# Order in which weight tiles are converted during the first output products, and the place of the first expert gather

## The chip, the cores and the metric

The kernel runs on one core of one Trainium2 chip. The metric is device time in microseconds for one execution, lower is better. TensorE (PE in the profile, PEld for its weight loads) does the matrix products, VectorE (DVE) and ScalarE (ACT) elementwise work, GpSimd (POOL) elementwise work on SBUF and indirect DMAs, and SyncE (SP) issues most of the direct DMAs. Each engine takes its instructions in a fixed order.

## The reference

Three parts in a row, all in float32:

```python
# attention over 32 memory slots: q, k, v [4, 8, 576, 64], phi [4, 8, 576, 32]
a = exp(phi - max over seq); a = a / (sum over seq + 1e-9)
k_m, v_m = einsum('bhsm,bhsd->bhmd', a, k), einsum('bhsm,bhsd->bhmd', a, v)
x = softmax(q @ k_m^T / 8) @ v_m          # then laid out as 2304 tokens x 512
# gated layer: w_gate, w_val [512, 1536], w_out [1536, 512], stored as float64
x = (silu(x @ w_gate) * (x @ w_val)) @ w_out
# experts: r_gate [512, 8], w1 [8, 512, 1024], w2 [8, 1024, 512]
e = argmax(x @ r_gate); each token goes to expert e, in order of tokens, up to its capacity
out = softmax weight of e * (relu(x @ w1[e]) @ w2[e]), zero where the capacity is used up
```

The three weights of the gated layer arrive as 64-bit numbers and have to be turned into pairs of 32-bit numbers on the chip (a high part and the rest). Every product is made of three passes over such pairs.

## The kernel before

**Groups of the gated layer.** The 1536 columns of the gated layer are 12 tiles of 128 (`ft` 0 to 11), in three thirds of four. The four batches are two pairs: LATE (2, 3) and (0, 1). The work is done in six groups (L61, L62): LATE with the first third, LATE with the second, (0, 1) with the first, (0, 1) with the second, (0, 1) with the last, LATE with the last. This text calls them group 0 to group 5. A group (`moe_group`, L1081) has an input phase of eight steps, one for each tile and batch (`moe_in`, PE L652, with the gate on ACT L660 and DVE L661 and L662, and its split into a pair on ACT L118 and POOL L122), and then the output products (`moe_out`, PE L673), four runs of four columns of products, with the result copied (L681) or added (L683) to `yp`. Before the steps of a tile its weights are multiplied with the attention memories (`mem_in`, PE L609 and L624, pair made on ACT L118 and DVE L122).

**Conversion of a weight tile.** `prep_load` (L540) loads the two raw halves of a tile of `w_gate` and `w_val` (512 KB each, SP, tag `wr` with four buffers, so two tiles). `split64` (L141) converts one half: ACT L149, DVE L150, L152 and L153, ACT L118, POOL L122. The result lies in a buffer of tag `w8` (five buffers, 1 MB each). The tiles of `w_out` go the same way (`out_load` L574, `out_made` L583; six tiles `o0` to `o5`, two for each third). A converted tile is also stored to DRAM (`wsc`, `osc`), because a later group needs it again; it is then loaded back by a POOL DMA (`prep_back` L569 at L571, `prep_out` L591 at L596).

**Which tile when.** `prep_to(i)` (L1058) makes tiles in the order of the groups, and loads the raw halves of the next one ahead. Group 0 converts tiles 0 to 3 and `o0`, `o1` in its input phase. During its output products it makes tile 4 (L1170), loads the raw halves of tile 5, and then (L1174 to L1181) converts tile 7, `o3` and `o2`, which are stored, let go and loaded back in group 1. Tiles 5 and 6 are converted in group 1.

**Order on the engines.** The instructions are put in order by a planner, which simulates the engines and takes, of the instructions that it thinks ready, the one that is earliest in the program, or has been given a higher priority. `behind()` (L127) opens a block in which each DVE or ACT instruction is put after the last gate made so far. `prep_made` (L561) and `out_made` use it for every conversion. The chip then follows that order, with its own times.

**Routing and experts.** In group 5 (and 4) each finished block of 288 tokens is routed (`route`, L690): logits, argmax, position; POOL scatters the token numbers to `perm` (L753) and SP stores the rows to `x2` (L779). At the start of group 5 `end_of_first` (L1211) finishes the routing of the four early blocks, makes a table of two full units of 288 tokens (`unit_table`), starts loading the first expert's weights and reads the token numbers of both units (`unit_slots`, L839). After the output products of the first LATE batch, in a `behind()` block, `begin_early` (L1199) makes the row indices (`slots_of`, DVE L850 and L851), gathers the first unit's 3 x 96 rows from `x2` (`unit_gather`, POOL L863), transposes them (`unit_x`, PE L911), converts expert weights and gathers the second unit. The rows of block 4 are stored to `x2` before this in the program, those of blocks 5 to 7 after it. Then the units follow (`unit_up` PE L925, `unit_down` PE L951).

Of the kernel before, what the change touches and what calls it, by code (L numbers as in the profile page):

```python
# [21 lines left out]
def attention_moe_moe_kernel(  # L22
# [27 lines left out]
    NDT = DM // 128  # L50
# [29 lines left out]
    def w8(shape, name, dt=F32R):  # L80
        return sb.tile(shape, dt, tag="w8", name=name, bufs=5)
# [45 lines left out]
    def behind():  # L127

        stack = ExitStack()
        for ins in last:  # L130
            stack.enter_context(tc.issue_after(ins.ins))
        return stack
# [107 lines left out]
    def advance(gen, n):  # L240
        for _ in range(n):
            if gen is None or next(gen, StopIteration) is StopIteration:
                return
# [296 lines left out]
    def prep_load(ft):  # L540
        raws = []
        for src in (w_gate, w_val):
            raw = wraw([128, NDT, 128, 2], "wr", I32)
            nc.sync.dma_start(
                raw.rearrange("p t f w -> p (t f w)"),
                src[:, ft * 128 : ft * 128 + 128].bitcast(I32).rearrange("(t p) f -> p t f", p=128),
            )
            raws.append(raw)
        return raws
# [9 lines left out]
    stored = set()  # L559

    def prep_made(ft, w, raws):  # L561
        with behind():
            for i in range(2):
                advance(prep_split(w, raws, i), ALL)
        if ft >= FG:
            prep_store(ft, w)
        return w
# [6 lines left out]
    def out_load(t):  # L574
        raws = []
        for i in range(2):
            raw = wraw([128, DM, 2], "wor", I32)
            r0 = (2 * t + i) * 128
            nc.sync.dma_start(raw.rearrange("p f w -> p (f w)"), w_out[r0 : r0 + 128].bitcast(I32))
            raws.append(raw)  # L580
        return raws

    def out_made(t, raws):  # L583
        w = w8([128, 2, 2, DM], "wo")
        with behind():
            for i in range(2):
                advance(split64(raws[i], w[:, i, 0], w[:, i, 1]), ALL)
        nc.sync.dma_start(osc[t].bitcast(F32), w.rearrange("p i a f -> p (i a f)").bitcast(F32))
        return w
# [269 lines left out]
    def unit_gather(st, slots):  # L859
        st["idx"], idg = slots  # L860
        xr = st["xr"] = txr([CH, NC, ROW], "xr")
        for c in range(NC):
            nc.gpsimd.indirect_dma_start(  # L863
                xr[:, c], None, x2, bass.IndirectOffsetOnAxis(idg[:, c : c + 1], 0)
            )
# [215 lines left out]
    def moe_group(g, gen):  # L1081

        bs, G = PAIRS[g], GROUPS[g]
        start = g == 0
        rt = None
        ghs = [[], []]
        fts = range(G * FG, (G + 1) * FG)
        if start:
            steps = [(i, ft) for i in range(2) for ft in fts]
        else:  # L1090
            steps = [(i, ft) for ft in fts for i in range(2)]
        ws = []
        first = g * FG
        mhs = {}

        jobs = {2: [8, 9, ("o", 4)], 3: [10, 11, ("o", 5)]}.get(g, [])
        job_raws = {}
        prep_to(first + (0 if start else LOOK))
        low = not start

        def memory(n):
            i, ft = steps[n]
            w = preps[first + ft - G * FG]
            if start:
                mhs[n] = first_mh.pop() if first_mh else mem_in(bs[0], w, (i,))[0]
            elif i == 0:
                mhs[n], mhs[n + 1] = mem_in(bs[0], w, (0, 1))

        memory(0)
        for n, (i, ft) in enumerate(steps):  # L1110
            if n + 1 < len(steps) and start:
                if n < FG:
                    prep_to(steps[n + 1][1])
                if n + 1 == FG:
                    advance(gen, ALL)
                    gen = both(0)
                    low = True
                memory(n + 1)
            if n + 3 >= len(steps) and len(ws) < 2:
                ws.append(prep_out(2 * G + len(ws)))  # L1120
            ghs[i].append(moe_in(bs[i], mhs.pop(n), g > 1))
            if start and i == 1:
                prep_store(ft, preps[ft])
            if not start and n + 2 < len(steps):
                memory(n + 2)
            if i == 1 and not start:
                prep_to(min(first + ft - G * FG + 1 + LOOK, first + FG))
            if n % 2 == 0 and n // 2 < len(jobs):
                job = jobs[n // 2]
                job_raws[job] = prep_load(job) if isinstance(job, int) else out_load(job[1])  # L1130
            if n % 2 == 1 and n // 2 < len(jobs):
                job = jobs[n // 2]
                if isinstance(job, int):
                    prep_made(job, w8([128, 2, NDT, 2, 128], "wgv"), job_raws[job])
                else:
                    out_made(job[1], job_raws[job])
                stored.add(job)
            with tc.high_priority(offset=50 if low else 0), (behind() if start and low else ExitStack()):
                advance(gen, 3 if (start and not low) or g == 5 else 1)
        if g == 1:  # L1140
            for i, b in enumerate(LATE):
                nc.sync.dma_start(asc[i].bitcast(F32), state[b]["at"].rearrange("p q a t -> p (q a t)").bitcast(F32))
        if g == 1:
            for i in range(NT // 128):
                pin(nc.sync.dma_start(
                    out[i * 128 : (i + 1) * 128].rearrange("p (t c) -> p t c", t=NDT),
                    zero.unsqueeze(1).to_broadcast([128, NDT, 128]),
                ))

            for i in range(NT // 256, NT // 128):  # L1150
                pin(nc.sync.dma_start(
                    x2[i * 128 : (i + 1) * 128, :DM].rearrange("p (t c) -> p t c", t=NDT),
                    zero.unsqueeze(1).to_broadcast([128, NDT, 128]),
                ))
                pin(nc.sync.dma_start(x2[i * 128 : (i + 1) * 128, DM:], zero[:, : ROW - DM]))
        if g == 4:
            for i, b in enumerate(LATE):
                at = state[b]["at"] = tb([128, 2, 2, 2 * NB], "at")
                nc.sync.dma_start(at.rearrange("p q a t -> p (q a t)").bitcast(F32), asc[i].bitcast(F32))
        if g == 5:  # L1160
            for i, b in enumerate(LATE):
                yps[b] = tb([128, 2, NDT, NB], "yp", F32)
                nc.sync.dma_start(yps[b].rearrange("p n d t -> p (n d t)"), ysc[i])
            advance(gen, ALL)
        for j, b in enumerate(bs):
            if G == 0:
                yps[b] = tb([128, 2, NDT, NB], "yp", F32)
            for n in range(2):
                if 2 * j + n < LOOK:
                    prep_to(first + FG + 2 * j + n)  # L1170
                for _ in moe_out(G, ghs[j], ws, yps[b][:, n], n):
                    advance(rt, 1)
                advance(rt, ALL)
                k = 2 * j + n - 1  # L1174
                if start and k == 0:
                    prep_made(2 * FG - 1, w8([128, 2, NDT, 2, 128], "wgv"), prep_load(2 * FG - 1))
                    stored.add(2 * FG - 1)
                elif start and k > 0:
                    t = 3 - (k - 1)
                    out_made(t, out_load(t))  # L1180
                    stored.add(("o", t))  # L1181
                with tc.high_priority(offset=50):
                    advance(gen, 1)
                if G == NG - 1:
                    rt = route(2 * b + n, yps[b][:, n])
            if g == 5 and j == 0:
                with behind():
                    begin_early()
            if g == 1:
                nc.sync.dma_start(ysc[j], yps[b].rearrange("p n d t -> p (n d t)"))  # L1190
        if g > 0:
            advance(gen, ALL)
        return rt, gen
# [2 lines left out]
    early = []  # L1196
    first_unit = []

    def begin_early():  # L1199
        slots = early.pop()  # L1200
        early.append(slots_of(slots, "e"))
        st = first_unit.pop()
        unit_gather(st, early[1][0])
        unit_x(st)
        unit_w1(st, 3)
        early.append(st)
        st = unit_begin(early[0], 1)
        unit_gather(st, early[1][1])
        early.append(st)
# [95 lines left out]
```

## Time and profile before

| what | value |
|---|---|
| time, median of 3 runs | 840.52 us (839.5 to 840.86) |
| time of the profiled execution | 835.02 us |
| span of its profile | 833.3 us |
| PE busy | 708.3 us, 85% of the span |
| DVE, ACT, POOL busy | 60%, 44%, 31% |

Times of the trace are microseconds from the start of the span. A row of a timeline gives the start, the duration, the engine, the line, the operation with its tiles, and in brackets how long the engine had been idle and what ended it. The granted clock is that of TensorE, as a share of its full 2.4 GHz.

### The profile page before, as it was taken

To read this page: it belongs to the slowest core of one execution; us is meant where nothing else is said; L and a number is where in the kernel's file an instruction comes from. 1 tells how busy PE (TensorE), PEld (TensorE's weight loads), DVE (VectorE), ACT (ScalarE), POOL (GpSimd) and SP (SyncE) were. 2 spreads that over 40 slices of the span, in tenths; PEclk is the share of its full clock that TensorE was granted. 3 is DMA by queue.
4 is the path that set the end of the run, shared out by engine and by line. 5 is a ranking of instruction groups with operands and counts; after the bars stand their busy time and mean duration, and the time that the engine had idled before them with its cause. 6 is when DMAs were issued, how large, how long until landed. Compare 5 with 4: busy or idle time off the path is not lost. (4 is left out here: it accounts for less than half of the span.)

```text
span 833.3 us, 14158 instructions
## 1 busy us (share of the span) xinstructions
PE 708.3 (85%) x5232; PEld 672.3 (81%) x5232; DVE 502.6 (60%) x1100; ACT 370.0 (44%) x763; POOL 254.2 (31%) x289
## 2 busy tenths in 40 slices
PE   6777689921889988988999999959699999999992
PEld 5557679911779978987999988949599999999992
DVE  4767868547645685187275687746446675547551
ACT  2444455424642465365073465426135544544440
POOL 1453353034622164055042154041134222111101
PEclk7767989975989999999999999979889999999997
DMA  9958299998951179067164498442329666546521
GB/s 231 239 173 219 76 274 347 295 217 280 373 163 57 58 274 332 2 208 297 54 217 147 107 190 161 152 138 62 69 76 339 245 207 208 187 162 205 181 77 31
DMA packets 91672, 152.69 MB, mean 183 GB/s; under 512 B 28815, under 2 KB 66319, under 8 KB 84816
## 3 DMA queue, kind: packets, MB, share of 16 engines
q1 hardware_dynamic: 83712, 113.68, 46.6%
q0 software_dynamic: 7888, 38.07, 14.5%
q8 instruction: 43, 0.70, 0.4%
q14 instruction: 29, 0.24, 0.1%
HBM read 111.48 MB, written 40.51 MB: 182 GB/s over the span
## 5 line engine op out<-in xcount | busy, mean ns | idle before, releaser
L673 PE MATMUL py<-gh,wo 128*128 128x288 f32 x1152 | 163.7, 298 | 3.7 <-DVE sg L661 3.0
L673 PEld LDWEIGHTS py<-gh,wo 128*128 128x128 f32 x1152 | 155.4, 188 | 6.0 <-DVE sg L661 3.5
L652 PE MATMUL pg<-at,mh 128*128 128x288 f32 x576 | 109.0, 316 | 20.8 <-DVE sg L661 8.6
L122 POOL TENSOR_TENSOR gh<-sg,gh 128x288 fp32r<-128x288 f32 x96 | 81.0, 855 | 112.6 <-ACT gh L118 112.2
L925 PE MATMUL p<-xt,w1h 128*128 128x288 f32 x768 | 111.8, 301 | 0.6 <-DVE hh L120 0.6
L652 PEld LDWEIGHTS pg<-at,mh 128*128 128x128 f32 x576 | 88.4, 200 | 28.6 <-DVE sg L661 9.8
L652 PE MATMUL pv<-at,mh 128*128 128x288 f32 x576 | 105.7, 309 | 4.9 <-DVE sg L662 4.1
L951 PE MATMUL p<-hh,w2h 128*128 128x288 f32 x768 | 108.4, 298 | 0.0
L925 PEld LDWEIGHTS p<-xt,w1h 128*128 128x128 f32 x768 | 104.9, 191 | 1.6 <-DVE hh L120 0.8
L951 PEld LDWEIGHTS p<-hh,w2h 128*128 128x128 f32 x768 | 103.1, 188 | 0.6 <-ACT w2h L118 0.3
L652 PEld LDWEIGHTS pv<-at,mh 128*128 128x128 f32 x576 | 89.2, 199 | 6.4 <-DVE sg L662 5.0
L122 DVE TENSOR_TENSOR w2h<-w2r,w2h 128x1024 fp32r<-128x1024 f32 x36 | 42.4, 1220 | 57.6 <-ACT w2h L118 56.5
L122 DVE TENSOR_TENSOR mh<-pm,mh 64x512 fp32r<-64x512 f32 (+1 forms) x92 | 63.1, 688 | 22.3 <-ACT mh L118 20.5
L661 DVE SCALAR_TENSOR_TENSOR sg<-sg,pg 128x288 f32<-128x288 f32 x96 | 42.2, 449 | 51.5 <-ACT sg L660 50.6
L624 PE MATMUL pm<-wgv,tv 128*128 128x256 f32 x288 | 43.9, 301 | 33.9 <-ACT wgv L118 33.7
L660 ACT ACTIVATE sg<-pg 128x288 f32<-128x288 f32 x96 | 38.2, 409 | 71.1 <-PE pg L652 51.4
L624 PEld LDWEIGHTS pm<-wgv,tv 128*128 128x128 f32 x288 | 39.7, 203 | 35.5 <-ACT wgv L118 33.9
L118 ACT ACTIVATE mh<-pm 64x512 fp32r<-64x512 f32 (+1 forms) x92 | 54.4, 592 | 27.9 <-PE pm L624 16.6
L136 POOL DMA_INDIRECT out_dram<-ot,idx x24 | 23.7, 989 | 118.0 <-DVE ot L967 113.4
L118 ACT ACTIVATE gh<-sg 128x288 fp32r<-128x288 f32 x96 | 41.2, 442 | 33.3 <-DVE sg L662 27.8
L683 DVE TENSOR_TENSOR yp<-py,yp 128x288 f32<-128x288 f32 x64 | 29.1, 456 | 41.3 <-PE py L673 41.0
L122 POOL TENSOR_TENSOR wgv<-mag,wgv 128x512 fp32r<-128x512 f32 x24 | 32.8, 1366 | 60.8 <-ACT wgv L118 57.0
(206 smaller groups left out, 1025.0 us busy)
## 6 DMA issues: line engine op xcount, KB each, us to landing
w1r<-in_moe_w_dram SPq DMA_DIRECT2D x36, 512.0 KB
w2r<-in_moe_w_dram SPq DMA_DIRECT2D x36, 512.0 KB
wgv<-wsc POOLq DMA_DIRECT2D x17, 1024.0 KB
wsc<-wgv SPq DMA_DIRECT2D x12, 1024.0 KB
wo<-osc POOLq DMA_DIRECT2D x10, 1024.0 KB
wr<-in_moe_w_gate_dram SPq DMA_DIRECT2D x12, 512.0 KB
wr<-in_moe_w_val_dram SPq DMA_DIRECT2D x12, 512.0 KB
wor<-in_moe_w_out_dram SPq DMA_DIRECT2D x12, 512.0 KB
```

The lines of the kernel that those rows point to most:

```text
L118: act = nc.scalar.activation(hi, src, AF.Relu if relu else AF.Copy)
L122: (nc.gpsimd if pool else nc.vector).tensor_sub(lo, src, hi.bitcast(F32))
L136: ins = nc.gpsimd.indirect_dma_start(*args, **kwargs)
L624: nc.tensor.matmul(pm[:, Q * 256 : (Q + 1) * 256], tv[:, 2 * Q + hp, a, :], w[:, c, 2 * Q + hp], start=(n3 == 0), stop=(n3 == 2),)
L652: nc.tensor.matmul(pg[gv][:, :NB], mh[:, a, Q, gv * 128 : gv * 128 + 128], at[:, Q, c, ns], start=(Q == 0 and n3 == 0), stop=(Q == 1 and n ...
L660: nc.scalar.activation(sg, pg[0][:, :NB], AF.Tanh, scale=0.5 / 256)
L661: nc.vector.scalar_tensor_tensor(sg, sg, 1.0, pg[0][:, :NB], ALU.add, ALU.mult)
L673: nc.tensor.matmul(py[:, :NB], ws[i // 2][:, i % 2, a, d * 128 : d * 128 + 128], gh[:, c, ns], start=(i == 0 and n3 == 0), stop=(i == len( ...
L683: nc.vector.tensor_add(yp[:, d], py[:, :NB], yp[:, d])
L925: nc.tensor.matmul(p1[:, :NB], st["w1"][d][:, a, f * 128 : f * 128 + 128], st["xt"][d][:, c], start=(d == 0 and n3 == 0), stop=(d == NDT - ...
L951: nc.tensor.matmul(p2[:, :NB], w2h[f // 2][:, f % 2, a, d * 128 : d * 128 + 128], hh[f][:, c], start=(f == 0 and n3 == 0), stop=(f == NF2 ...
```

## The change

During the output products of group 0 the tiles 4, 5 and 6 are made, in the order in which group 1 uses them; tile 7, `o2` and `o3` are made in group 1 itself and not loaded back there. The conversions of tiles below 4 are no longer put behind the last gate. The row indices of both early units and the first gather stand before the output products of group 5 and are no longer in a `behind()` block; the rest of `begin_early` stays where it was.

```diff
     def prep_made(ft, w, raws):
-        with behind():
+        with behind() if ft >= FG else ExitStack():
             for i in range(2):
                 advance(prep_split(w, raws, i), ALL)
...
             advance(gen, ALL)
+            early_slots()
         for j, b in enumerate(bs):
...
                 k = 2 * j + n - 1
-                if start and k == 0:
-                    prep_made(2 * FG - 1, w8([128, 2, NDT, 2, 128], "wgv"), prep_load(2 * FG - 1))
-                    stored.add(2 * FG - 1)
-                elif start and k > 0:
-                    t = 3 - (k - 1)
-                    out_made(t, out_load(t))
-                    stored.add(("o", t))
+                if start and 0 <= k < 2:
+                    prep_to(first + FG + k + 1)
...
-    def begin_early():
+    def early_slots():
         slots = early.pop()
         early.append(slots_of(slots, "e"))
+        unit_gather(first_unit[0], early[1][0])
+
+    def begin_early():
         st = first_unit.pop()
-        unit_gather(st, early[1][0])
         unit_x(st)
```

## Rows read from the trace of the kernel before

**Rows 1.** The page, the span in 40 slices of 20.8 us: the rows of PE (busy tenths; the first digit is slice 0) and of its granted clock (tenths).

```profile
PE   6777689921889988988999999959699999999992
...
PEclk7767989975989999999999999979889999999997
```

**Rows 2.** The view of the waits: engine, line and tile, what it waited for, us in total, times, the longest.

```profile
PE pm L624 <- ACT wgv L118: 33.7, 1, 33.7
...
PE pxt L911 <- DMA xr<-x,idg: 9.0, 3, 4.2
...
PE pm L609 <- ACT wgv L118: 7.5, 2, 6.2
```

**Rows 3.** The view by windows: start and end, length, busy us of PE, PEld, DVE, ACT and POOL, then granted clock, DMA share and GB/s.

```profile
140.00:160.00 20.00, 20.00 (x148) 19.58 (x147) 10.79 (x17) 6.71 (x16) 1.30 (x1) 1.00 1.07 308
161.40:205.50 44.10, 8.93 (x63) 7.88 (x61) 26.80 (x42) 16.23 (x30) 13.73 (x11) 0.67 0.98 247
161.40:252.10 90.70, 49.18 (x376) 44.13 (x375) 53.91 (x99) 40.53 (x85) 37.62 (x40) 0.77 0.86 251
279.60:324.30 44.70, 37.72 (x266) 35.91 (x265) 36.77 (x69) 30.08 (x62) 22.07 (x26) 0.96 0.68 242
348.00:391.80 43.80, 36.72 (x269) 34.90 (x268) 36.19 (x65) 28.05 (x60) 22.85 (x26) 1.00 0.59 207
548.00:559.40 11.40, 2.37 (x14) 1.58 (x13) 2.91 (x5) 1.76 (x4) 8.62 (x9) 0.66 0.71 197
```

**Rows 4.** The timeline of PE in group 1's input phase: the last product of tile 4, the first attention product of tile 5, the first output products.

```profile
170.85 0.96 PE L652 MATMUL pv<-at,mh 128*128 128x288 f32 x6
...
205.48 0.79 PE L624 MATMUL pm<-wgv,tv 128*128 128x256 f32 x2 [33.67 <-ACT wgv L118]
...
252.10 14.83 PE L673 MATMUL py<-gh,wo 128*128 128x288 f32 x110
```

**Rows 5.** The timeline of ACT in the same stretch: the first step of the conversions of tile 7, `o3` (185.47), `o2` (191.78) and tile 5.

```profile
163.63 0.68 ACT L149 ACTIVATE mag<-wr 128x512 f32<-128x512 f32 x1
...
185.47 0.66 ACT L149 ACTIVATE mag<-wor 128x512 f32<-128x512 f32 x1 [10.13 <-DMA wor<-in_moe_w_out_dram]
...
191.78 0.67 ACT L149 ACTIVATE mag<-wor 128x512 f32<-128x512 f32 x1 [0.34 <-DMA wor<-in_moe_w_out_dram]
...
198.79 0.65 ACT L149 ACTIVATE mag<-wr 128x512 f32<-128x512 f32 x1
```

**Rows 6.** The timeline of SP: the raw loads of tile 5 (first half, 139.36), tile 7 (second half, 158.73), `o3` and `o2`.

```profile
139.36 0.62 SPq L544 DMA_DIRECT2D wr<-in_moe_w_gate_dram  x1
...
158.73 1.46 SPq L544 DMA_DIRECT2D wr<-in_moe_w_val_dram  x1
...
180.05 1.74 SPq L579 DMA_DIRECT2D wor<-in_moe_w_out_dram  x2
...
188.07 3.06 SPq L579 DMA_DIRECT2D wor<-in_moe_w_out_dram  x2
```

**Rows 7.** The groups by line: DVE's three steps for a half of a tile (busy us, mean ns of one).

```profile
L153 DVE SCALAR_TENSOR_TENSOR mag<-mag,wr 128x512 int32<-128x512 int32 x24 | 21.6, 901 | 0.7
L152 DVE SCALAR_TENSOR_TENSOR wr<-wr 128x512 int32<-128x512 int32 x24 | 19.2, 799 | 0.5
...
L150 DVE TENSOR_SCALAR wr<-mag 128x512 int32<-128x512 int32 x24 | 15.4, 640 | 13.5 <-ACT mag L149 13.4
```

**Rows 8.** The page: DMA issues of the loads back.

```profile
wgv<-wsc POOLq DMA_DIRECT2D x17, 1024.0 KB
...
wo<-osc POOLq DMA_DIRECT2D x10, 1024.0 KB
```

**Rows 9.** The timelines around the first gather: SP reads the token numbers, DVE makes the indices, SP stores the rows of block 4, ACT converts the fourth tile of `w1`, POOL issues the first gather, PE starts on the first unit.

```profile
517.96 1.07 SPq L839 DMA_DIRECT2D idx<-perm  x2
...
542.57 0.17 DVE L850 TENSOR_SCALAR valid<-idx 96x6 f32<-96x6 int32 x1
...
542.72 0.34 SPq L779 DMA_DIRECT2D x<-rows  x1
...
547.29 2.00 ACT L118 ACTIVATE w1h<-w1r 128x1024 fp32r<-128x1024 f32 x2 [6.17 <-PE py L673]
...
547.42 0.95 POOL L863 DMA_INDIRECT xr<-x,idg  x1 [23.69 <-DVE drop L749]
...
559.40 1.33 PE L925 MATMUL p<-xt,w1h 128*128 128x288 f32 x4
```

**Rows 10.** The timelines in the input phase of group 0: ACT's first step for tile 2, SP's last load of attention input, PE's wait for tile 2 and its next attention product, and PE's wait for the second batch of LATE.

```profile
59.51 1.23 ACT L149 ACTIVATE mag<-wr 128x512 f32<-128x512 f32 x2
...
62.28 0.31 SPq L267 DMA_DIRECT2D kvraw<-in_v_dram  x1
...
66.67 0.58 PE L609 MATMUL pm<-wgv,tv 128*128 128x256 f32 x1 [6.16 <-ACT wgv L118]
...
67.83 2.35 PE L346 MATMUL kvp<-kvraw,ex 112*32 112x128 f32 x38
...
104.98 0.61 PE L652 MATMUL pg<-at,mh 128*128 128x288 f32 x1 [3.68 <-ACT at L118]
```

**Rows 11.** The view of the waits, of SP's queue.

```profile
SPq L579 <- DVE mag L153: 61.7, 6, 35.7
...
SPq L839 <- DMA perm<-tokid,addr: 8.0, 1, 8.0
```

## Prediction

> **What bounds the kernel now.** The page comes first: TensorE is busy for 85% of the span, and its 40 slices show where the rest lies. From slice 10 on most digits are 9, but slices 8 and 9 (166 to 208 us) hold 2 and 1, and slice 26 (542 to 562) holds 5; the granted clock falls in the same places [rows 1]. PE is thus the bound, except in a few stretches where it waits. The view of the waits names them: 33.7 us in one piece for a converted weight tile in `mem_in`, 9.0 us in three pieces for gathered rows, 7.5 us for tiles of group 0, 6.2 of it in one piece [rows 2]. All three are of the kind that the change touches. The windows show what the other engines do meanwhile [rows 3], the timelines of PE, ACT and SP in which order [rows 4 to 6, 9, 10].
>
> In the longest one PE ends tile 4's products at 170.85 + 0.96 = 171.8 and starts tile 5's at 205.48 [rows 4]. ACT's row shows why: after tile 4 it converts tile 7, then `o3`, `o2`, and only at 198.79 tile 5 [rows 5], though tile 5's raw loads were issued from 139.36 on [rows 6], 59 us before. The tile needed next is converted fourth, and `o3` and `o2` are themselves late, because their raw loads go out at 180.05 and 188.07 [rows 6].
>
> **The change part by part.**
>
> *Group 1.* Tiles 5 and 6 take the place of 7, `o3` and `o2` in the output products of group 0; 7, `o2` and `o3` come in group 1. No conversion is saved: 12 + 6 tiles are converted and stored as before. One load back of tile 7 and two of `o2`, `o3` go, 3 of 27 [rows 8], 3 MB.
> The stall of 33.7 us goes when tile 5 is converted before 171.8. Its raw data are asked for at 139.36, its conversion took from 198.79 until PE could start at 205.48 [rows 4, 5], 7 us, and between 140 and 160 DVE was busy for 10.8 of 20 us, ACT for 6.7, POOL for 1.3 [rows 3]. That is the cover: PE's output products, which need ACT for one copy per run only. I take tile 5 as ready by 160.
> Tile 6 then stands where tile 7 stood (raw load 158.73, conversion from 163.63 [rows 5, 6]), ready at about 175; PE needs it after the products of tiles 4 and 5, no earlier than 176 (8 us of PE a tile: 43.8 - 7 us of idle in group 3's phase, over four tiles, is 9).
> What is late next is the rest of the phase. Before, it ran from 161.4 to the first output product at 252.1: 90.7 us [rows 3, 4]. Without the stall it would be 57.0. From DVE's side: its 53.9 us of work there lose one tile, 2 x (0.90 + 0.80 + 0.64) = 4.7 us [rows 7], and leave 49.2. The input phases of groups 2 and 3, which also convert three tiles each, kept DVE busy for 36.77 / 44.70 = 82% and 36.19 / 43.80 = 83% [rows 3]; at that share 49.2 us of DVE need 60 us. Bounds: 49 (DVE without a gap) and 90.7 (no gain). I take 60.7, nearest to groups 2 and 3: 30 us less. A little of that is clock, which stood at 0.67 from 161.4 to 205.5 and pays back when PE no longer idles.
> DMA is the resource that I can't read to the end. The phase moved 251 GB/s x 90.7 us = 22.8 MB with the DMA engines busy 0.86 of the time [rows 3]. Without 3 MB, 19.8 MB in 60.7 us are 326 GB/s; the row before the phase reached 308 at a share of 1.07, the phase itself 247 at 0.98 [rows 3]. The Trainium skill, Perfetto Trace Analysis, section Roofline, gives about 435 GB/s for a core's 16 DMA engines together; by that 19.8 MB need an estimated 46 us and DMA bounds nothing here, while the rows of this trace, at full share with 250 to 310 GB/s, speak against so much.
>
> *First gather.* Before, the indices are made at 542.57, SP stores block 4's rows at 542.72, POOL's gather starts at 547.42 [rows 9], and PE waits 9.0 us for its three parts [rows 2]. Two DVE instructions and three POOL issues move; none is added. The token numbers were asked for at 517.96 [rows 9], so the data allow a gather some 20 us earlier, and the new place in the program frees it from block 4's store and from the `behind()` block. POOL has nothing else to do then: it idled 23.7 us before the gather [rows 9]. Queued behind the moved instructions are, on DVE, gates and additions to `yp`, on POOL, the splits of the last gates.
> All 9.0 us gone: PE starts the unit at 559.4 - 9.0 - 1 (transposes at half clock, 2.37 us busy in 11.4 at 0.66 [rows 3]) = 549.4. What is late then is the fourth tile of `w1`, which ACT and DVE convert from 547.29, when the last output products release its buffer [rows 9], until about 549.7; it costs nothing more. Lower bound: the planner put the indices at 542.57 although the numbers were long there, so it may believe them late; then only the wait for the store goes, 547.42 - 543.5 = 3.9 us. Below nothing: indices placed among the last gates, before the numbers land, would hold DVE; SP itself waited 8.0 us for the scatters to `perm` [rows 11]. Ends -8 and +10; I take +8, nearer to the full wait.
>
> *Group 0 without `behind()`.* PE waits 6.16 us for tile 2, whose conversion starts at 59.51, right behind a gate [rows 10] and begins with both raw halves at once, so that both had landed. Gain at most 6.2 at that place. But the attention product behind it needs a load issued at 62.28 and started at 67.83 [rows 10], and the second batch's steps wait for attention until 104.98 [rows 10], so part is given back. On the other side a conversion that slips in front of the softmax on DVE costs about its 4.7 us. Ends -5 and +6; I take +3.
>
> Sum: 30 + 8 + 3 = 41. The profiled execution took 835.0 us, 1.7 of it outside the span of 833.3, and 5.5 less than the median of 840.5. It would take 794.0; the median 799.5.
>
> **The rivals.**
>
> *DMA bounds group 1.* The DMA engines' busy time in the phase is 0.86 x 90.7 = 78 us; 3 MB less at 251 / 0.86 = 292 GB/s take off 10.5 and leave 67.5, and at a share of 0.93 that is 72.5 us of phase. The gain there is 18 instead of 30: 840.5 - 18 - 11 = 811.5. For it: shares of 0.98 and 1.07 in the rows. Against: the stall was not DMA's, tile 5 lay in SBUF; and the loads for group 2 can wait for the output products.
>
> *Tiles in order, but placed late.* The planner puts tile 5 where tile 7 was (163.63 on), behind the output products. PE then waits from 171.8 to 175, and each later tile (6, 7, `o2`, `o3`) follows 11.7 us after the one before, the pace from tile 7 to tile 5 ((198.79 - 163.63) / 3 [rows 5]), until 222; with attention's products the output products start near 230. Phase 68.5, gain 22, time 840.5 - 22 - 11 = 807.5. For it: ACT was busy for a third of the time from 140 to 160 [rows 3] and tile 7 was not put there; against: its second raw half was issued at 158.73 only, tile 5's first at 139.36 [rows 6].
>
> *The gather brings nothing or blocks.* Sum 30 + 3 with -8 to +4: 803.5 to 815.5, middle 810. For it the lower bounds above; against, DVE and POOL have idle places after the last gate.
>
> *Slower: the raw loads of group 1 form a chain on SP.* `o2`'s loads wait for a pair of raw buffers that tile 6 must leave, `o3`'s for tile 7's, and SP waits in order. Once this queue waited 35.7 us for a buffer of that kind [rows 11]. If 7 and then `o3` each wait like that, the phase takes 49 + 2 x 35.7 = 120 us, 30 more than before, and the time is 840.5 + 30 - 11 = 859.5. It makes the kernel slower from a phase of 90.7 + 11 + 1.7 = 103.4 us on. Against: in the trace four tiles in a row (7, `o3`, `o2`, 5) went through in 42 us although they shared two of the four buffers; at that pace the new chain ends near 206, before PE needs it.
>
> **How the numbers follow.** The forecast has 0.5, DMA 0.18, late placement 0.13, the gather 0.13, the slower case 0.03; 0.03 is left for no change by some other give-back. What a measurement of this kernel can tell from no change is about 0.2%. Faster by more than that: 0.94; within: 0.02; slower: 0.04. The forecast's own range is 788 to 808: group 1 from 24 to 36, gather 4 to 10, group 0 from 0 to 6. Towards the top the range takes in the DMA and gather cases up to 818; towards the bottom a phase of 52 us with both other gains full, 840.5 - 38.7 - 16 = 786.
>
> **What would show it.** Right: no wait of over 10 us before `pm`; ACT converting in the order 4, 5, 6, 7, `o2`, `o3`, with tile 5 before 161; the first output product of group 1 some 60 us after group 0's last; 16 and 8 loads back; the first gather well before the end of group 5's output products, and no wait of `pxt` for it; tile 2 converted before PE asks. Wrong: DMA share near 1 through group 1 with PE waiting for attention's inputs (the DMA rival); tile 5 after the copies of `yp` (late placement); DVE idle ahead of `valid` (blocked); SP waiting long for raw buffers (slower). The prediction is wrong as a whole if group 1's phase stays over 80 us.

## The result, and the profile after

The changed kernel takes 803.2 us (median of 4 runs, 801.8 to 809.4) beside 840.0 of the kernel before; the ratio is 0.9575, with an interval of 0.9524 to 0.9627. The forecast was 799.5, its range 786 to 818, with faster at 0.94. The profiled execution took 802.25 us, its span 800.4 us, 32.9 less than before.

The page of the changed kernel, 40 slices of 20 us each: busy tenths of PE, granted clock, share of the DMA engines.

```profile
PE   6769688988899979979999989896999999999992
PEclk9858989999889989999999999997999999999996
DMA  9959399999932592276451878543179655746421
```

The hole of [rows 1] in slices 8 and 9 is filled. Slices 5 to 10 of the DMA row, 100 to 220 us, all read 9: there the DMA engines are busy for 90% of the time or more, and this row turned out to be the one to weigh more.

Windows of the changed kernel: group 0's output products, group 1's input phase, and the first part of group 1's output products (us; busy time of each engine with instruction counts; granted clock; DMA share; GB/s).

```profile
121.69:159.79 38.10, 36.14 (x272) 33.44 (x271) 27.32 (x45) 18.67 (x46) 9.54 (x8) 0.96 1.08 302
159.79:221.92 62.13, 50.11 (x377) 44.06 (x375) 48.48 (x95) 36.87 (x82) 33.64 (x35) 0.91 0.98 289
221.92:252.14 30.22, 30.22 (x200) 29.80 (x201) 14.58 (x33) 4.03 (x9) 4.38 (x4) 0.90 0.24 89
```

The phase that took 90.7 us in [rows 3] takes 62.1. The output products ahead of it took 33.8 us before and 38.1 now. Those behind it took 27.5 and now take 30.2, with PE busy throughout in both but a granted clock of 0.90 instead of 1.00 (behind a wait of 2.6 us a part runs at the lower of the two levels, 1.2 GHz), so that 2.8 us of the gain are given back there. The rows of before, of the same columns:

```profile
127.57:161.40 33.83, 33.52 (x273) 31.98 (x271) 20.75 (x37) 15.24 (x39) 6.30 (x5) 1.00 1.07 332
252.10:279.56 27.46, 27.46 (x204) 27.04 (x203) 15.37 (x35) 4.72 (x10) 4.39 (x4) 1.00 0.11 44
```

PE's timeline in the phase (start, duration, line, operation, count, and the idle time ahead of it with what ended it), which answers to [rows 4]: tiles 4 and 5 in one run of 24 products, tile 6, tile 7, and the first output product. Tile 5 is not among the waits at all.

```profile
159.79 3.01 PE L624 MATMUL pm<-wgv,tv 128*128 128x256 f32 x24
...
173.38 0.70 PE L624 MATMUL pm<-wgv,tv 128*128 128x256 f32 x2 [2.50 <-ACT wgv L118]
...
197.53 1.46 PE L624 MATMUL pm<-wgv,tv 128*128 128x256 f32 x10 [0.77 <-POOL wgv L122]
...
221.92 2.29 PE L673 MATMUL py<-gh,wo 128*128 128x288 f32 x8 [2.63 <-DVE sg L661]
```

ACT's first step of each conversion, as in [rows 5]: two for tile 5, the first of tile 6, then tile 7, `o2` and `o3`. The order is the one in which PE needs them.

```profile
145.54 0.67 ACT L149 ACTIVATE mag<-wr 128x512 f32<-128x512 f32 x1 [0.48 <-DMA wr<-in_moe_w_gate_dram]
...
152.83 0.67 ACT L149 ACTIVATE mag<-wr 128x512 f32<-128x512 f32 x1 [0.69 <-DMA wr<-in_moe_w_val_dram]
...
162.03 0.67 ACT L149 ACTIVATE mag<-wr 128x512 f32<-128x512 f32 x1
...
188.01 1.21 ACT L149 ACTIVATE mag<-wr 128x512 f32<-128x512 f32 x2
...
195.20 0.66 ACT L149 ACTIVATE mag<-wor 128x512 f32<-128x512 f32 x1
...
209.37 1.20 ACT L149 ACTIVATE mag<-wor 128x512 f32<-128x512 f32 x2
```

The loads back, which answer to [rows 8]:

```profile
wgv<-wsc POOLq DMA_DIRECT2D x16, 1024.0 KB
wo<-osc POOLq DMA_DIRECT2D x8, 1024.0 KB
```

The first gather, which answers to [rows 9]: DVE makes the indices 44 us earlier and POOL gathers 48 us earlier, 27.4 us of both because the last group's output products start so much earlier, and PE no longer waits for gathered rows. In its place stands a new wait, for the pair of `xr` buffers: the second unit's gather, from 525.76 on, fills one, the rows of the next block need the other, and there the store of the rows before, issued at 535.98, is in the way until 550.3.

```profile
498.62 0.17 DVE L850 TENSOR_SCALAR valid<-idx 96x6 f32<-96x6 int32 x1 [3.63 <-DMA idx<-perm]
...
499.87 1.68 POOL L863 DMA_INDIRECT xr<-x,idg  x1 [3.51 <-DVE idg L851]
...
535.98 0.33 SPq L779 DMA_DIRECT2D x<-rows  x1
...
550.29 1.55 ACT L778 COPY rows<-pw 96x512 f32<-96x512 f32 x3 [12.39 <-DMA x<-rows]
...
550.92 1.14 PE L696 MATMUL pl<-yh,rg 128*16 128x288 f32 x4 [7.77 <-ACT rows L778]
```

By starts, before and after: group 1's first output product 252.10 and 221.92 (30.2 earlier), group 2's input phase 279.56 and 252.14 (27.4), group 5's output products 519.26 and 491.88 (27.4), the first unit's products 559.40 and 529.60 (29.8), the second's 606.50 and 573.14 (33.4). From there on the two kernels run alike.

### The profile page after: what moved, and what is told of

Read it like the earlier page. It is cut to its first block, busy times and chain, and to the rows that moved or that the text cites. A ratio compares the mean times of both kernels' runs of the same rounds, so it can differ in the third digit from the quotient of the medians.

```text
span 800.4 us, 14138 instructions
## 1 busy us (share of the span) xinstructions
PE 709.9 (89%) x5232; PEld 674.0 (84%) x5232; DVE 502.7 (63%) x1100; ACT 366.2 (46%) x763; POOL 257.7 (32%) x286
## 5 line engine op out<-in xcount | busy, mean ns | idle before, releaser
L673 PE MATMUL py<-gh,wo 128*128 128x288 f32 x1152 | 172.4, 305 | 6.9 <-DVE sg L661 5.6
L673 PEld LDWEIGHTS py<-gh,wo 128*128 128x128 f32 x1152 | 161.8, 195 | 10.3 <-DVE sg L661 6.7
L652 PE MATMUL pg<-at,mh 128*128 128x288 f32 x576 | 108.4, 316 | 20.6 <-DVE sg L661 8.0
L661 DVE SCALAR_TENSOR_TENSOR sg<-sg,pg 128x288 f32<-128x288 f32 x96 | 41.9, 449 | 49.6 <-ACT sg L660 48.9
L122 DVE TENSOR_TENSOR w1h<-w1r,w1h 128x1024 fp32r<-128x1024 f32 x36 | 42.9, 1220 | 11.7 <-ACT w1h L118 11.5
L118 ACT ACTIVATE w2h<-w2r 128x1024 fp32r<-128x1024 f32 x36 | 36.4, 1053 | 24.1 <-DMA w2r<-in_moe_w_dram 13.9
```

Source lines behind the costliest of these rows:

```text
L118: act = nc.scalar.activation(hi, src, AF.Relu if relu else AF.Copy)
L122: (nc.gpsimd if pool else nc.vector).tensor_sub(lo, src, hi.bitcast(F32))
L652: nc.tensor.matmul(pg[gv][:, :NB], mh[:, a, Q, gv * 128 : gv * 128 + 128], at[:, Q, c, ns], start=(Q == 0 and n3 == 0), stop=(Q == 1 and n ...
L661: nc.vector.scalar_tensor_tensor(sg, sg, 1.0, pg[0][:, :NB], ALU.add, ALU.mult)
L673: nc.tensor.matmul(py[:, :NB], ws[i // 2][:, i % 2, a, d * 128 : d * 128 + 128], gh[:, c, ns], start=(i == 0 and n3 == 0), stop=(i == len( ...
```

## Experiments

The change has three parts, and the first four runs take them one by one. All times are medians, each ratio is against runs of the kernel before on the same chip (837 to 841 us); "phase" is group 1's, from tile 4's `pm` to the first output product in the profiled execution.

**The order alone.** The hunk of the output products, with `behind()` everywhere and the gather in its old place:

```diff
-                if start and k == 0:
-                    prep_made(2 * FG - 1, w8([128, 2, NDT, 2, 128], "wgv"), prep_load(2 * FG - 1))
...
+                if start and 0 <= k < 2:
+                    prep_to(first + FG + k + 1)
```

> The kernel before with the tile order alone: tiles 5 and 6 are prepared in group 0's output products, 7, o2 and o3 in group 1; behind() and the place of the first gather as before. If the stall of 33.7 us was the order and nothing else, PE's wait for tile 5 is gone, group 1's phase falls from 90.7 to about 62 us as in the changed kernel, and the time is 840.5 - 28.6 = 812. If the free placement of group 1's conversions (no behind()) is what lets tile 5 in early, tile 5 is converted only after the output products, the phase stays at some 68 us or more, and the time is 818 or above.

820.5 us, ratio 0.9754 (0.9698 to 0.981): 20.6 us of 840, where 28.6 were expected if the stall was the order and nothing else. The stall is gone (2.5 us are left ahead of tile 6), but the phase takes 72.3 us. Tile 5 is converted from 145.3 on, so "placed late" is not the reason.

```profile
160.18:232.43 72.25, 53.20 (x377) 47.61 (x375) 51.53 (x95) 37.28 (x83) 34.18 (x35) 0.86 0.92 269
```

**`behind()` away for tiles 0 to 3 alone.**

```diff
-        with behind():
+        with behind() if ft >= FG else ExitStack():
```

> The kernel before with behind() taken away for tiles 0 to 5 alone. If what group 0 gains is given back in its own output products, the first output product comes about 6 us earlier, the last of group 0 under 2 us earlier, the stall for tile 5 stays near 33 us, and the time is 838 to 841. If the 6 us are kept to the end, as the upper bound of the prediction has it, 834.

841.4 us, ratio 1.0022 (0.9989 to 1.0056): nothing. (The expectation speaks of tiles 0 to 5; the edit frees tiles 0 to 3.) PE's timeline shows both halves: tile 2 makes PE wait 0.5 us instead of 6.2 [rows 10], but tile 1 now costs 4.2 and the load of attention's inputs 3.7, so that the first output product starts at 127.28 instead of 127.57.

```profile
38.09 0.58 PE L609 MATMUL pm<-wgv,tv 128*128 128x256 f32 x1 [4.17 <-ACT wgv L118]
...
52.24 0.58 PE L609 MATMUL pm<-wgv,tv 128*128 128x256 f32 x1 [0.54 <-ACT wgv L118]
...
124.55 0.64 PE L346 MATMUL kvp<-kvraw,ex 112*32 112x128 f32 x4 [3.70 <-DMA kvraw<-in_v_dram]
```

**The early gather alone.**

```diff
+            early_slots()
...
-    def begin_early():
+    def early_slots():
         slots = early.pop()
         early.append(slots_of(slots, "e"))
+        unit_gather(first_unit[0], early[1][0])
...
-        unit_gather(st, early[1][0])
```

> The kernel before with the early indices and the early first gather alone. If the gather's wait of 9.0 us goes and nothing comes in its place, the time is 840.5 - 8 = 832.5. If the early gather only moves the wait to the store of the second block's rows, about half is left: 836 to 837. If the indices block DVE among the last gates, 841 or above.

828.3 us, ratio 0.9853 (0.9795 to 0.991): 12 us, more than any of the three cases had, with the 7.6 of the interval's upper end near the profile's own 7.7 (span 825.6 against 833.3). The wait for gathered rows is gone, and the one for the rows' buffer is there:

```profile
PE pl L696 <- ACT rows L778: 9.1, 1, 9.1
```

**Order and gather, `behind()` back.**

```diff
-        with behind() if ft >= FG else ExitStack():
+        with behind():
```

> The changed kernel with behind() back for all tiles: the new order and the early gather alone. If the parts add up, it loses only what is left of group 0's gain, 1.6 us: 803.2 + 1.6 = 805. If the new order needs the free placement, tile 5 or 6 is late and the time is 810 or above. If the free placement costs in group 0's output products as much as it brought, 802 to 804.

806.4 us, ratio 0.9617 (0.9553 to 0.968): between the first and the second case, and the intervals of this and of the changed kernel overlap. The phase takes 70.4 us. DVE's timeline near its end shows `o3`'s conversion (L152, L153) standing between the gates' steps (L661, L662), and PE behind them:

```profile
216.16 1.89 DVE L152 SCALAR_TENSOR_TENSOR wor<-wor 128x512 int32<-128x512 int32 x1
217.97 0.44 DVE L661 SCALAR_TENSOR_TENSOR sg<-sg,pg 128x288 f32<-128x288 f32 x1
218.34 3.43 DVE L153 SCALAR_TENSOR_TENSOR mag<-mag,wor 128x512 int32<-128x512 int32 x1
221.69 0.44 DVE L662 SCALAR_TENSOR_TENSOR sg<-sg,pv 128x288 f32<-128x288 f32 x1
...
222.18 1.81 PE L652 MATMUL pv<-at,mh 128*128 128x288 f32 x6 [2.66 <-DVE sg L662]
```

**Order and free placement, gather in its old place.**

```diff
-            early_slots()
...
-        unit_gather(first_unit[0], early[1][0])
...
+        unit_gather(st, early[1][0])
```

> The changed kernel with indices and first gather back in their old place: the new tile order and tiles 0 to 3 without behind(). If the early gather is worth the 8 us of the prediction, 803.2 + 8 = 811. If it is worth the 12 to 14 us by which the medians with and without it differed so far, 815 to 817. Group 1's phase should be 62 us as in the changed kernel, not the 70 to 72 us that it took wherever behind() stood for tiles 0 to 3.

812.7 us, ratio 0.966 (0.9581 to 0.9739): 9.5 us more than the changed kernel, near the first case. But 5.4 of the 9.0 us by which the profile comes later to the second unit are there before the last group's output products, so the medians alone don't size the gather. The stretch that it acts on, from the last group's first output product to the second unit's first product, does: it took 84.8 to 88.4 us in the six profiles with the gather in its old place (mean 86.4) and 77.6 to 81.5 us in the five with the early gather and the `xr` pair as it is (mean 79.3). By them the gather brings 7.1 us.

The phase missed: 67.3 us, though up to there the instructions stand in the same order as in the changed kernel. So its 62.1 was one of the shorter executions of that order; the run with the rows in other buffers, below, had 63.9. The mean of the three is 64.4, and what `behind()` costs the phase beside the zero writes (below) is then 7 us (72.3 and 70.4, again two executions of one order, have a mean of 71.3).

**`o3` asked for one step later**, with `behind()` for tiles 0 to 3:

```diff
-            if n + 3 >= len(steps) and len(ws) < 2:
+            if n + 3 - 2 * len(ws) >= len(steps) and len(ws) < 2:
```

> The kernel with the new order and the early gather but behind() for tiles 0 to 3, with o3's preparation asked for one step later, so that its two raw loads of 0.5 MB go to SP behind the loads of attention's next inputs. If those raw loads ahead of kvraw are what made the phase 70 us, PE's wait of 4.5 us for kvraw goes, the phase is 63 to 66 us and the time 806.4 - 4.5 = 802. If it is something else that behind() holds up, 805 to 808.

799.7 us, ratio 0.9514 (0.9441 to 0.9587), phase 62.9. The time came near the first case, 802, though the interval overlaps that of the run without this edit (0.9553 to 0.968); the mechanism did not: `o3`'s raw loads still go out first, and PE still waits for `kvraw`, 5.6 us instead of 4.5.

```profile
201.27 0.64 PE L346 MATMUL kvp<-kvraw,ex 112*32 112x128 f32 x4 [5.60 <-DMA kvraw<-in_v_dram]
```

What moved is the conversion: its first step on ACT starts at 217.70 instead of 212.75, behind most of the gates, and DVE is busy for 45.1 us of the phase instead of 51.5. The theory of the loads fell. What the two timelines show in its place is `o3`'s conversion on DVE ahead of the gates; PE's waits for gates in the phase fell from 8.8 to 5.2 us, so that this explains 3.6 of the 7.5 us, and the rest is not taken apart.

**The rows in buffers of their own.** This tests the new wait of 7.8 us.

```diff
-        rows = txr([CH, NC, ROW], "rows")
+        rows = traw([CH, 2, ROW], "rows")
+        row2 = t2k([CH, ROW], "row2")
...
```

> The changed kernel with the routed rows built in two other kinds of buffer (two thirds in a raw tile, one third in a t2k tile) instead of the pair that the gathered rows also use; stores become two each. If the wait of 7.8 us in the first unit is for that pair alone, ACT's 12.4 us and PE's 7.8 us are gone and the time is 795.4, with PE held by the next late thing perhaps 797 to 799. If the second unit's gather or the last gates are as late as the buffer, the wait only changes its name: 802 to 804.

795.3 us, ratio 0.947 (0.9392 to 0.9548). The forecast of 795.4 held. The stretch from the last group's output products to the second unit takes 70.7 us instead of 81.3, and the longest wait of PE between 480 and 575 us is now

```profile
PE pl L696 <- ACT yh L118: 1.6, 1, 1.6
```

**The zero writes later.** This tests the rival that DMA bounds group 1.

```diff
-        if g == 1:
+        if g == 3:
             for i in range(NT // 128):
                 pin(nc.sync.dma_start(out[...], zero...))
```

> The changed kernel with the zero writes of out and of half of x2, 4.72 + 2.38 = 7.1 MB, moved from the end of group 1 to the end of group 3 in the program. If DMA bounds group 1's phase (the DMA rival: share 1.0 at some 290 GB/s), 7.1 MB less take up to 24 us of DMA away there, the phase falls under 57 us and the time under 798. If DVE, ACT and PE's order bound it, the phase stays at 60 to 62 us and the time at 802 to 804. If the writes hurt where they go to, above 805.

791.3 us, ratio 0.9428 (0.9355 to 0.9502). The rival was right in part. The phase takes 57.3 us with a DMA share of 0.68. Group 0's output products take 32.2 us instead of 38.1, but they start 4.0 us later, with 39 of PE's products already done (x233 instead of x272), and end 2.0 us earlier. From group 3's output products to those of the last group, where the writes now are, nothing is lost (131.0 us in both, 354.11 to 485.11 here, 360.93 to 491.88 in the changed kernel).

```profile
125.64:157.81 32.17, 32.15 (x233) 30.97 (x234) 28.08 (x51) 19.14 (x48) 12.84 (x10) 1.00 1.06 327
157.81:215.13 57.32, 46.80 (x376) 42.16 (x374) 47.77 (x87) 34.84 (x78) 29.73 (x33) 0.93 0.68 214
```

Not all of the 11.9 us are the writes'. In the profiles 6.8 us are gained up to group 1's first output product (215.13 instead of 221.92). Another 4.4 us come in the last group's output products, where neither kernel has zero writes and the engines' order is the same: the changed kernel's profiled execution has the wait of 2.6 us for `yh` at 510.28 there. The run with `behind()` back, in the same order and with its writes in the old place, was as short as this one. The changed kernel, this run and that run:

```profile
491.88:529.60 37.72, 35.10 (x264) 33.71 (x262) 24.44 (x78) 17.23 (x35) 9.77 (x10) 0.95 0.49 147
485.11:518.46 33.35, 33.35 (x263) 32.23 (x262) 24.83 (x78) 16.85 (x36) 9.80 (x10) 1.00 0.53 166
498.65:532.15 33.50, 33.50 (x263) 32.27 (x262) 24.36 (x78) 16.84 (x36) 9.75 (x10) 1.00 0.49 156
```

Over all executions of the two orders, group 1's first output product starts at 221.92, 227.89 and 225.57 with the writes and at 215.13 and 216.14 without, 9.5 us between the means. So moving the writes is worth some 7 to 10 us. The edit also lets the planner place other instructions of groups 0 and 1 anew (some 300 of PE's 1294 up to the end of the phase), so that the bytes on the DMA engines, the queue on SP and the new order are not told apart.

Two runs then ask how much of the first result was the writes.

**The zero writes later, in the kernel before** (the same edit):

```diff
-        if g == 1:
+        if g == 3:
```

> The kernel before with the zero writes at the end of group 3 and nothing else. If the stall of 33.7 us was ACT's order of conversions alone, the writes lay in its shade: at most the 4 to 6 us at group 0's output products, 835 to 840. If DMA had a part in the stall, as the DMA rival would have it, about 12 us: 828.

821.9 us, ratio 0.9822 (0.9774 to 0.987): 15 us, and this is the run that corrects my reading most. With the conversions in their old order, the stall of 33.7 us shrinks to 14.0:

```profile
185.20 0.80 PE L624 MATMUL pm<-wgv,tv 128*128 128x256 f32 x2 [13.98 <-ACT wgv L118]
```

SP shows why. The raw loads of `o3` and `o2`, which went out at 180.05 and 188.07 [rows 6], are asked for 22 to 31 us earlier, as the queue has no zero writes in front of them; here too the planner placed other instructions anew:

```profile
148.89 0.38 SPq L579 DMA_DIRECT2D wor<-in_moe_w_out_dram  x1
...
157.48 0.35 SPq L579 DMA_DIRECT2D wor<-in_moe_w_out_dram  x1
...
162.38 7.97 SPq L579 DMA_DIRECT2D wor<-in_moe_w_out_dram  x2
```

The phase still takes 80.7 us: new waits for a gate (7.6) and for `kvraw` (4.9) take a part back.

**The order alone, with the zero writes later.**

```diff
+                if start and 0 <= k < 2:
+                    prep_to(first + FG + k + 1)
...
-        if g == 1:
+        if g == 3:
```

> The kernel before with the new tile order and the zero writes at the end of group 3; behind() and the place of the gather as before. If the zero writes are what kept the order's own gain at 20 us instead of 30, the phase falls from 72 to about 60 us and the time from 820.5 to 808 to 810. If behind() for tiles 0 to 3 holds up the conversions whatever DMA does, the phase stays over 68 us and the time over 814.

800.4 us, ratio 0.9541 (0.9491 to 0.959), below both cases: the phase takes 56.1 us, with `behind()` for all tiles. Without the writes `behind()` thus costs the phase nothing that shows (57.3 and 58.1 with the free placement).

```profile
159.08:215.15 56.07, 46.45 (x376) 42.69 (x375) 46.61 (x86) 34.35 (x77) 30.88 (x33) 0.93 0.66 211
```

**Both edits on the changed kernel, and `o3` later as well.** The diffs are those of the single edits.

```diff
+        rows = traw([CH, 2, ROW], "rows")
...
+        if g == 3:
```

> The changed kernel with both single edits that helped it: the rows in buffers of their own and the zero writes at the end of group 3. The two act in stretches 250 us apart; if they add up, 803.2 - 7.9 - 11.9 = 783.4. If the first unit's stall comes back because everything ahead of it is earlier, 787 to 791.

787.6 us, ratio 0.9407 (0.9361 to 0.9452): the rows bring 3.7 us on top of the zero writes, not 7.9. PE no longer waits for them, but from the last group's output products to the second unit it takes 76.4 us against 70.7 with the rows alone, among other things for three waits of 1.8 to 2.3 us. The order is not the reason: in this stretch PE and DVE have the same instructions in the same order as in the run with the rows alone. The executions differ, as the six times from 784.0 to 794.0 do; why is open. The three profiles with the rows in their own buffers (70.7, 76.4 and, with `o3` later, 72.3) have a mean of 73.1, 6.2 us below the 79.3 of the shared pair.

```diff
+            if n + 3 - 2 * len(ws) >= len(steps) and len(ws) < 2:
```

> The kernel with both edits and o3's preparation asked for one step later. If o3's conversion ahead of the gates on DVE still holds PE up at the end of group 1's phase, 2 to 4 us less than with both alone: 779 to 781. If the phase without the zero writes has room for it, no difference: 783 to 784.

784.2 us, ratio 0.9352 (0.9313 to 0.9391), the best of all: 3.4 us less than with two edits, with intervals that overlap. The phase takes 52.9 us.

```profile
160.68:213.55 52.87, 44.94 (x377) 41.31 (x375) 42.10 (x83) 33.72 (x76) 27.98 (x32) 0.97 0.56 181
```

## Why the prediction was right, and where not

The total held; the terms did not all. Of the 41 us of the sum 36.8 came by the medians and 32.9 by the two profiles. The 0.2% that I gave a measurement of this kernel was too little: the runs of the kernel before went from 832.8 to 844.6.

*Group 1, 30 us.* What was to show it is there: no long wait ahead of `pm`, ACT in order with tile 5's last split at 155.75, 16 and 8 loads back, the first output product 62.1 us after group 0's last (60.7 forecast). In the profile this is 28.6 us, which is partly luck: over three executions of the same order the phase was 64.4 us, a gain of 26, and as a part by itself, with `behind()` where it was, the order brought 20.6 us by the ratios. The step that failed is the bound: "at that share 49.2 us of DVE need 60 us". DVE's busy time was sized well (48.5). But the share of 82% came from phases with a DMA share of 0.59 to 0.68, and beside the zero writes no run reached it: 78% in the changed kernel, 71 to 78% in the five other runs of the new tile order that have the writes there. In the four without them DVE is busy for 80 to 83% of the phase, so there the bound agrees with the rows. The same work then takes 56 to 58 us, and with `o3`'s conversion moved as well 53. What I called "the resource that I can't read to the end" was worth some 7 to 10 us of the changed kernel: 36 of the DMA issues from 100 to 168 us are zero writes of 7.1 MB that nobody needs before the first rows are stored at 438.9. My DMA sum took the phase's 22.8 MB as given and never asked which of them had to be there. A smaller slip: tile 6 was ready at 173.3, near the 175 forecast, but PE asked for it at 170.9 and not at 176 or later, hence the wait of 2.5 us.

The diagnosis was incomplete in the same way. "The tile needed next is converted fourth" is true and the change cures it; but I also wrote that `o3` and `o2` are late because their raw loads go out at 180.05 and 188.07, and did not ask why. They stood behind zero writes on SP. In the run with those moved some 20 of the 33.7 us are gone, though the phase is only 10 us shorter. Order and writes made the stall together, and undoing either took away most of it.

*First gather, 8 us.* Mechanism right, all 9.0 us of waits gone and nothing blocked on DVE: it waits 3.6 us for the numbers, and PE's only new wait ahead of the first unit is 2.6 us for a copy of `yh` at 510.28. By the profile it is 7.2 us (33.4 earlier at the second unit, against the 26.2 that both kernels differ by at group 4's output products, 444.00 and 417.80) and 7.7 in the run of that part; by the stretches it acts on 7.1. The medians of the pairs with and without it differ by 9.5 to 14, but the profiles of two of the three pairs also differ by 5 us ahead of the stretch. The term was sized well. What I named as late next, the fourth tile of `w1`, was not: the `xr` pair was, 7.8 us at 550.9, and the prediction did not follow what the second unit's rows, sitting in one of two buffers, do to the other user of the pair. The net loss is small, since a wait of 6.4 us that PE had at 601.69 for a step of the routing on DVE (`ohb`, L730) is gone.

*Group 0, 3 us.* Alone it brought nothing, as the lower half of its bounds allows: the place where part was to be given back, the load of attention's inputs, took it. In the changed kernel the first output product starts 5.9 us earlier and the last one ends 1.6 us earlier; the 4.3 us between went into group 0's output products, where PE is idle for 2.0 us instead of 0.3 (1.4 of it for attention's `qt`, 0.5 for `wo`) and has a clock of 0.96 instead of 1.00. In the two other executions of this order the first output product starts 2.9 and 2.4 us earlier, and the last ends 0.9 us earlier and 0.3 later. What it is worth in the sum, 3.5 us by the ratios with the early gather (the intervals overlap) and 7.9 without it, shows in group 1's phase, where the written order of `o3`'s conversion and the gates changes with it: a size that agrees and a cause that does not.

*Rivals.* "DMA bounds group 1" was wrong in its time for the whole change (phase 72.5; the order alone came to 72.3, at a share of 0.92) and right in part of its cause; "placed late" fell, tile 5 was converted ahead of the last output products; the gather did not block; SP's chain of raw loads did not form (`o3`'s went out at 193.6). The Trainium skill, Perfetto Trace Analysis, section Roofline, gives about 435 GB/s for a core's 16 DMA engines. By that figure DMA bounded nothing in group 1. The windows shown here at a share near 1 moved 289 to 332 GB/s, and the runs without the writes speak against it.

## To carry to other kernels

When a tile is late, follow each load ahead of it back to its queue, and for everything that stands in front of it ask when its result is needed: fillers that cost nothing in a slack stretch can hold half of a stall that looks like an order of conversions. When a phase runs at a DMA share near 1, count which of its bytes must move there, and don't size it by an engine's share from phases with less DMA. And before a difference of medians is put down to an edit, look in which stretch of the profile it arises, and whether the edit acts there. When a step is moved forward, look at how long its buffer is now held and who else draws on the same pair.

## What the runs showed of the hardware

The same DVE step on a 128x512 tile (L153) took, in the run with `behind()` back, 0.67 us at its shortest, 0.87 and 1.02 on the mean of its two groups, and 3.43 in one place; POOL's timeline shows it splitting `at` at the same time and issuing loads:

```profile
217.44 1.10 POOL L571 DMA_DIRECT2D wgv<-wsc  x2
218.56 1.43 POOL L122 TENSOR_TENSOR at<-af,at 128x576 fp32r<-128x576 f32 x1
219.94 1.26 POOL L122 TENSOR_TENSOR wo<-mag,wo 128x512 fp32r<-128x512 f32 x1
```

Whether POOL is the cause was not tried. The issue of a zero write to `out` on SP took 0.55 to 4.97 us, and the 36 zero writes together 35.5 us of SP's queue in the changed kernel (the three durations are least, median and most, in ns; the changed kernel, then the one with the writes moved):

```profile
L1145 SPq DMA_DIRECT2D out_dram<-zero x18: 546/872/4965, 100.7 to 131.5; - x18
```

```profile
L1145 SPq DMA_DIRECT2D out_dram<-zero x18: 642/868/3022, 358.7 to 377.8; - x18
```

A store of 580 KB of rows held its buffer for 14.3 us (535.98 to 550.29) beside gathers, scatters and weight loads.
